# Two transformer-like layers in float32r on one core: first tile in two runs of chunks, the sum of phi(k) in float32r, accumulators added one by one

## Chip, cores and metric

The kernel runs on one core of a Trainium2 chip. The metric is the device time of one execution in microseconds (us). Three runs of the kernel before took 1350.85, 1351.03 and 1351.11 us; their median is 1351.03.

## What is computed

The input is one sequence of 2048 rows with 640 columns. Two kinds of block alternate, A, B, A, B, each on a layer-normalized copy and with a residual. A is linear attention with 32 heads of 20 columns; B is a feed-forward block of width 1728 with a squared ReLU.

```python
def _A_ref(x, wqkv, wo):
    q, k, v = split_heads(x @ wqkv)              # 32 heads of 20
    phi = lambda t: jnp.where(t > 0, t + 1, jnp.exp(t)) + 1e-6
    pq, pk = phi(q), phi(k)
    kv = jnp.einsum("bhsd,bhse->bhde", pk, v)
    z = jnp.einsum("bhsd->bhd", pk)              # the sum of phi(k)
    num = jnp.einsum("bhqd,bhde->bhqe", pq, kv)
    den = jnp.einsum("bhqd,bhd->bhq", pq, z)[..., None] + 1e-6
    return merge_heads(num / den) @ wo

def _B_ref(x, w1, b1, w2, b2):
    h = x @ w1 + b1
    r = jnp.where(h > 0, h, 0)
    return (r * r) @ w2 + b2

for _ in range(2):
    x = x + _A_ref(_layernorm(x), A_wqkv, A_wo)
    x = x + _B_ref(_layernorm(x), B_w1, B_b1, B_w2, B_b2)
```

## The kernel before

Rows are worked in 16 tiles of 128, columns in 5 chunks of 128. Most matmuls are in float32r. Every operand of these is split into a high part (float32r) and a low part (the rest), and a product is three matmuls, high with low, low with high, high with high (`mm3`, line 377). `split` (line 127) makes the high part on ScalarE (ACT) and the low part on VectorE (DVE).

**The order is written out by hand.** `tc.manual_schedule()` keeps each engine's instructions in the order in which the Python code issues them. All DMAs but one of the last tile stand in one queue, that of SyncE (SP). TensorE (PE) writes into the eight banks of PSUM, which the code hands out by number.

**Start of layer 0.** PE is kept busy with filler transposes (`warm`, line 521: 30, and 15 more behind the first tile's). Tile 0 is loaded, normalized (`a_stats`, `a_apply`; 1/sigma is made on GpSimd, POOL), transposed by PE (`a_trans`) and split (`xT_split`). Meanwhile `FirstLoads` (line 165) brings in the ten blocks of the k and q weights, five chunks of each, and splits each block as `step` asks for it. The first tile then has a loop of its own in stage A (line 681): for k and then for q, for each chunk, for each half of 320 columns, one `mm3`. Between, at q's chunk 2, PE transposes tile 1.

**Stage A.** For each tile the K and Q projections are made (`part`, line 460), phi is applied in `Phi` (line 471: `exp` on ACT, the rest on DVE in `rest`), phi(k) is split (`k_post`, line 645) and added up in `acc` on POOL, and PE multiplies it with the normalized input into G (`g_part`, five banks) and into GT (`gt_part`, in pairs of tiles, added up on DVE). For some tiles the q projection is put off (`LATE`, `late_q`). At the end of stage A the sum of phi(k) over the rows is a matmul of a 128x128 tile of ones with `acc`, in float32 (line 806); its result on all partitions, `zbc`, gives the denominators.

**Stage B and the feed-forward stage.** G is turned into one matrix per layer (`kv_make`, `m_make`), tiles 0 to 3 are finished, and then four groups of four tiles go through the feed-forward stage (line 1510). A step is one of 14 column blocks of a group: `fc1` (15 matmuls of 512 columns), `act` (ACT and DVE), and `fc2` of the step before (`fc2`, line 1114), which accumulates over the 14 steps in one bank for each tile (`a0` to `a3`) and one for the last 128 columns of all four (`as`, the strip). In the last step of a group the accumulators are added to the residual by DVE (`tile_add`, line 1106), and the next group's first matmul into such a bank waits for that. Work for the next groups' tiles hangs on places between these steps ("pre", 0 to 4, "pe", "post"); `single` (line 1379) lays it out for tiles 4 to 7, among it `f_bias` (line 631), which adds the second bias and stores the tile for the end of its group.

## Time and profile before

| | |
|---|---|
| runs | 1350.85, 1351.03, 1351.11 us |
| profiled execution | 1350.55 us |
| its span, from the first to the last instruction | 1348.6 us |
| DMA | 253.44 MB, mean 188 GB/s |

A row of the timeline has the start in us, the time from the first start to the last end in us, the engine, the line, the operation, what it writes and reads by the program's names, the shape and the count, and in brackets how long the engine was idle before and what ended that. PEld is the loading of weights into PE, SPq the issue of a DMA. In the view of waits a row has the waiting engine and line, what it waited for, the total in us, how often, and the longest. In a table by stretches of time each engine has its busy time and, with x, its number of instructions, and then the granted PE clock, the DMA share and GB/s. In the list of groups a row ends with the busy time in us and the mean of one instruction in ns, then the idle time before it.

### The profile page before, as it was taken

Reading aid. Unit: us, or ns where it says so; the run is one execution under the profiler, and the core shown is the slowest. Engines: PE = TensorE matmul, PEld = TensorE weight load, DVE = VectorE, ACT = ScalarE, POOL = GpSimd, SP = SyncE. Lnnn points to the kernel's source line nnn. Section 1 sums busy time; section 2 is a strip of 40 time slices with the busy share of each in tenths; the row PEclk is TensorE's granted clock in tenths of the full one; section 3 lists DMA queues with packets and bytes.
Section 4 is the critical chain, followed back from the end, with each engine's and each line's share of the span. In section 5 each row is a group of like instructions: output and inputs, shape, how many; then the busy total and the mean of one; then the engine's idle time right before and its main releaser. Section 6 shows DMA issues by size and latency. Waiting matters only on the chain.

```text
span 1348.6 us, 19071 instructions
## 1 busy us (share of the span) xinstructions
PE 1340.0 (99%) x6793; PEld 1157.7 (86%) x6793; DVE 914.9 (68%) x1631; ACT 796.9 (59%) x2021; POOL 122.6 (9%) x174
## 2 busy tenths in 40 slices
PE   9999999999999999999999999999999999999998
PEld 8888998988888888888888899988888888888887
DVE  7888757777776776643467676677778667766323
ACT  5888858566547447511647688485756466474120
POOL 2222210000000000000012232100000000000000
PEclk9999999999999999999999999999999999999999
DMA  6787824574654574487621114156546556545735
GB/s 205 254 295 270 287 91 167 191 287 136 216 205 161 200 263 166 154 298 291 224 98 49 50 40 150 47 206 247 175 164 228 179 176 224 208 163 181 252 128 194
DMA packets 85636, 253.44 MB, mean 188 GB/s; under 512 B 11030, under 2 KB 19606, under 8 KB 84902
## 3 DMA queue, kind: packets, MB, share of 16 engines
q1 hardware_dynamic: 85398, 252.04, 53.8%
q8 instruction: 54, 0.88, 0.3%
q14 instruction: 40, 0.33, 0.1%
q10 hardware_dynamic: 144, 0.20, 0.0%
HBM read 193.50 MB, written 56.03 MB: 185 GB/s over the span
## 4 chain that ended last, share of the span: by engine, by line
PE 89%; DVE 5%; ACT 3%; issue 1%; DMA 1%; POOL 0%; SPq 0%; DVEq 0%; ACTq 0%
PE PS L381 34%; PE PS L1057 27%; PE PS L1007 27%; ACT z L367 2%; PE PS L854 1%; PE PS L867 1%; DMA st<-in_A_wqkv_dram 0%; DVE bn L338 0%; DVE e L484 0%; DVE xr L623 0%; DVE r L485 0%; DVE xTb L130 0%; DMA Mr<-Mc 0%; POOL rs L343 0%; DVE y L358 0%
## 5 line engine op out<-in xcount | busy, mean ns | idle before, releaser
L367 ACT ACTIVATE z<-y 32x160 f32<-32x160 f32 x1424 | 475.8, 334 | 77.4 <-DVE y L358 61.2
L1007 PE MATMUL PS<-xTb,u 128*128 128x512 f32 x1400 | 333.1, 389 | 1.0 <-DVE xTb L130 1.0
L1007 PEld LDWEIGHTS PS<-xTb,u 128*128 128x128 f32 x1400 | 262.0, 188 | 55.3 <-DVE xTb L130 1.5
L381 PE MATMUL PS<-kq,xT 128*128 128x320 f32 (+2 forms) x1635 | 294.0, 334 | 1.4 <-DVE kq L130 0.9
L381 PEld LDWEIGHTS PS<-kq,xT 128*128 128x128 f32 x1635 | 259.0, 188 | 29.1 <-DVE kq L130 1.1
L1057 PE MATMUL PS<-u,h 128*128 128x512 f32 x1120 | 277.1, 390 | 0.3 <-DVE x L1108 0.3
L1057 PEld LDWEIGHTS PS<-u,h 128*128 128x128 f32 x1120 | 208.4, 188 | 41.9 <-DVE x L1108 1.2
L1019 ACT ACTIVATE hr<-PS,b1sb 128x512 f32<-128x512 f32 x104 | 71.4, 687 | 277.3 <-PE PS L1007 276.4
L1020 DVE TENSOR_TENSOR hr<-hr 128x512 f32<-128x512 f32 x104 | 71.8, 690 | 220.7 <-ACT hr L1019 220.3
L381 PE MATMUL PS<-kh,xh 128*128 128x512 f32 x480 | 124.3, 392 | 0.0
L477 ACT ACTIVATE e<-PS 128x320 f32<-128x320 f32 (+4 forms) x128 | 53.6, 435 | 102.6 <-PE PS L381 98.9
L342 POOL TENSOR_SCALAR rs<-mv 128x1 f32<-128x1 f32 x64 | 28.0, 438 | 869.8 <-DVE mv L340 869.8
L381 PE MATMUL PS<-uM,pT 128*128 128x320 f32 x648 | 102.6, 309 | 0.7 <-DVE uM L883 0.7
L381 PEld LDWEIGHTS PS<-uM,pT 128*128 128x128 f32 x648 | 97.7, 188 | 3.1 <-DVE uM L883 1.3
L381 PEld LDWEIGHTS PS<-kh,xh 128*128 128x128 f32 x480 | 87.3, 188 | 15.1
L484 DVE TENSOR_SCALAR e<-e 128x320 f32<-128x320 f32 (+4 forms) x128 | 41.2, 322 | 80.3 <-ACT e L477 80.0
L1057 PE MATMUL PS<-h,u 128*128 128x512 f32 x280 | 79.0, 390 | 0.0
L1022 DVE TENSOR_TENSOR h<-hr,h 128x512 fp32r<-128x512 f32 x104 | 72.0, 693 | 3.6
L652 POOL TENSOR_TENSOR acc<-acc,r 128x640 f32<-128x640 f32 x30 | 53.9, 1795 | 199.9 <-DVE r L485 199.9
L1057 PEld LDWEIGHTS PS<-h,u 128*128 128x128 f32 x280 | 52.1, 188 | 10.8 <-DVE h L1033 0.4
L1007 PE MATMUL PS<-xTb,uw 128*128 128x512 f32 x240 | 57.0, 389 | 0.0
L485 DVE SCALAR_TENSOR_TENSOR r<-PS,e 128x512 f32<-128x512 f32 (+2 forms) x104 | 51.1, 492 | 5.8 <-ACT e L477 2.4
(122 smaller groups left out, 1361.5 us busy)
## 6 DMA issues: line engine op xcount, KB each, us to landing
u<-kept_w SPq DMA_DIRECT2D x184, 640.0 KB, 4.5
x<-x SPq DMA_DIRECT2D x48, 320.0 KB, 4.8
kept_w<-uprep SPq DMA_DIRECT2D x23, 640.0 KB, 4.5
pqt<-pq SPq DMA_DIRECT2D x32, 320.0 KB, 4.6
x<-xr SPq DMA_DIRECT2D x32, 320.0 KB, 3.2
st<-in_B_w_dram SPq DMA_DIRECT2D x22, 320.0 KB, 5.9
pq<-r SPq DMA_DIRECT2D x20, 320.0 KB
kept_kq<-kq SPq DMA_DIRECT2D x10, 640.0 KB, 6.9
```

Source lines behind the costliest of these rows:

```text
L342: nc.gpsimd.tensor_scalar(rs, mv[:, 1:2], LN_EPS, None, op0=ALU.add)
L367: nc.scalar.activation(zv[j * B32 : (j + 1) * B32, :, i, :], yv[i * B32 : (i + 1) * B32, :, j, :], AF.Copy)
L381: nc.tensor.matmul(ps, a, b, start=first and i == 0, stop=last and i == 2)
L477: nc.scalar.activation(self.e[:, a:b], ps, AF.Exp)
L484: nc.vector.tensor_scalar(e, e, 1.0, PHI_EPS, op0=ALU.min, op1=ALU.add)
L485: nc.vector.scalar_tensor_tensor(out=self.r[:, a:b], in0=ps, scalar=0.0, in1=e, op0=ALU.max, op1=ALU.add)
L652: nc.gpsimd.tensor_tensor(out=acc, in0=acc, in1=r, op=ALU.add)
L1007: nc.tensor.matmul(ps, a[:, d, :], bb[:, d, :], start=d == 0 and i == 0, stop=d == DC - 1 and i == len(seq) - 1,)
L1019: nc.scalar.activation(r, ps, AF.Relu, bias=b1sb[:, c : c + 1])
L1020: nc.vector.tensor_tensor(out=r, in0=r, in1=r, op=ALU.mult)
L1022: nc.vector.tensor_tensor(out=h[:, 1], in0=r, in1=h[:, 0].bitcast(F32), op=ALU.subtract)
L1057: nc.tensor.matmul(ps, l, r, start=first and k == 0, stop=last and k == len(a) - 1)
```

## The change

Four edits are made together.

1. **The first tile in two runs of chunks.** Chunks 0 and 1, then 2 to 4, are normalized, transposed into two banks and split as separate instructions. There are 25 filler transposes instead of 30, and none behind the tile's transposes. The first tile's projections run chunk by chunk through k and q: the matmuls of both parts of the input with the weight's high part first, and those with the weight's low part two chunks later (`LAG`). Tile 1's transposes come at step 7 of this (`AT_T`), the first 512 columns of tile 1's projections at step 9 (`AT_P`), into bank 6. The statistics and normalizations of tiles 1 to 3, the last two q weights' splits and tile 2's transposes are moved accordingly.
2. **The sum of phi(k) in float32r.** `acc` is split like any operand, between the first two parts of the put-off q projections, and the sum is four float32r matmuls, the low part first, instead of two in float32. The tile of ones becomes float32r, written by DVE from a one-column constant, which shares a tile with the constant -0.5; POOL wrote it before.
3. **Accumulators added at once in a group's last step.** `tile_add` of a tile is issued right behind that tile's last `fc2` matmuls and not behind all four.
4. **The bias of tile 7** (`f_bias` for i = 3) comes one step later.

```diff
@@ -36,7 +36,10 @@
 LATE = ((9, 11, 12, 13, 14, 15), (8, 9, 11, 13, 14, 15))
 
 PREP = {t: 2 if t > 5 else 3 for t in range(2, 12)}
-N_WARM, N_WARM_2 = 30, 15
+N_WARM = 25
+
+
+LAG, AT_T, AT_P = 2, 7, 9
 AHEAD = 2
 F_BUFS = 12
 
@@ -107,7 +110,9 @@
 
     ident = cpool.tile([P, P], F32, name="ident")
     make_identity(nc, ident)
-    neghalf = cpool.tile([P, 1], F32, name="neghalf")
+    scalars = cpool.tile([P, 2], F32, name="scalars")
+    neghalf, one = scalars[:, 0:1], scalars[:, 1:2]
+    nc.vector.memset(one, 1.0)
     nc.vector.memset(neghalf, -0.5)
     b2bc = cpool.tile([P, D], F32, name="b2bc")
     b1sb = cpool.tile([P, NF], F32, name="b1sb")
@@ -169,16 +174,29 @@
             self.todo = [(nm, c) for nm in ("k", "q") for c in range(DC)]
             self.pending = []
 
+            self.halves = []
+
+        def high(self, n):
+            for _ in range(min(n, len(self.pending))):
+                (nm, c), raw = self.pending.pop(0)
+                if nm == "k":
+                    kq[c] = wtile("kq").rearrange("p (j n) -> p j n", j=2)
+                    keep(("kq", c), [P, 2, 2 * D])
+                s = slice(0, D) if nm == "k" else slice(D, 2 * D)
+                u = kq[c][:, :, s]
+                nc.scalar.activation(u[:, 0], raw, AF.Copy)
+                self.halves.append((u, raw))
+
+        def low(self, n):
+            for _ in range(min(n, len(self.halves))):
+                u, raw = self.halves.pop(0)
+                nc.vector.tensor_tensor(
+                    out=u[:, 1], in0=raw, in1=u[:, 0].bitcast(F32), op=ALU.subtract
+                )
+
         def finish(self):
-            if not self.pending:
-                return
-            (nm, c), raw = self.pending.pop(0)
-            if nm == "k":
-                kq[c] = wtile("kq").rearrange("p (j n) -> p j n", j=2)
-                keep(("kq", c), [P, 2, 2 * D])
-            s = slice(0, D) if nm == "k" else slice(D, 2 * D)
-            u = kq[c][:, :, s]
-            split(u[:, 0], u[:, 1], raw)
+            self.high(1)
+            self.low(1)
 
         def step(self, n=1, ahead=2):
             for i in range(n + 1):
@@ -527,18 +545,39 @@
             first_loads.step(0, 5)
             a_load(1, src)
             a_stats(0)
-            a_apply(0)
+            first_loads.high(2)
+
+            mv, rs = sts.pop(("a", 0))
+            T4[0] = tmp.tile([P, TG, 2, D], R32, tag="T", name="xT", bufs=2)
+            xT[0] = chunks(T4[0][:, 0])
+            runs = [(bank(4), 0, 2), (bank(5), 2, DC)]
+            for ps, a, b in runs:
+                v = xt[0][:, a * P : b * P]
+                nc.vector.tensor_scalar(v, v, mv[:, 0:1], rs, op0=ALU.subtract, op1=ALU.mult)
+            for ps, a, b in runs:
+                for c in range(a, b):
+                    nc.tensor.transpose(
+                        ps[:, (c - a) * P : (c - a + 1) * P], xt[0][:, c * P : (c + 1) * P], ident
+                    )
+                d = T4[0][:, 0, 0, a * P : b * P]
+                nc.scalar.activation(d, ps[:, : (b - a) * P], AF.Copy)
+            first_loads.low(1)
+            for ps, a, b in runs:
+                d = T4[0][:, 0, :, a * P : b * P]
+                nc.vector.tensor_tensor(
+                    out=d[:, 1], in0=ps[:, : (b - a) * P], in1=d[:, 0].bitcast(F32), op=ALU.subtract
+                )
+            first_loads.low(1)
             first_loads.step(2, 5)
-            a_trans(0, bank(4, 2))
-            warm(N_WARM_2)
-            first_loads.step(4, 5)
             a_stats(1)
+            first_loads.step(2, 5)
+            a_apply(1)
+            a_load(2, src)
             first_loads.step(1, 5)
-            a_apply(1)
-            first_loads.step(3, 5)
-            a_load(2, src)
-        ones = ap.tile([P, P], F32, name="ones", tag="ones", bufs=1)
-        nc.gpsimd.memset(ones, 1.0)
+            first_loads.high(1)
+            first_loads.low(1)
+        ones = ap.tile([P, P], R32, name="ones", tag="ones", bufs=1)
+        nc.vector.tensor_copy(ones, one.to_broadcast([P, P]))
         mask = ap.tile([HR, 6, DH], F32, name="mask", tag="mask", bufs=1)
         nc.gpsimd.memset(mask, 1.0)
 
@@ -680,26 +719,43 @@
                 load_vo(2 * t - 25)
             if first:
                 fk, fq = Phi(rtile()), Phi(rtile())
-                for nm, f, pss in (("k", fk, (bank(0), bank(1))), ("q", fq, (bank(2), bank(7)))):
-                    w = wk(nm)
-                    for c in range(DC):
+                pss = {"k": (bank(0), bank(1)), "q": (bank(2), bank(7))}
+
+                def first_part(nm, c, passes):
+
+                    x, w = xT[0][:, :, c, :], wk(nm)[c]
+                    for i in passes:
+                        k, l = ((0, 0), (1, 0), (0, 1))[i]
                         for j in range(2):
-                            s = slice(j * HD, (j + 1) * HD)
-                            mm3(
-                                pss[j][:, :HD], xT[t][:, 0, c, :], xT[t][:, 1, c, :],
-                                w[c][:, 0, s], w[c][:, 1, s], c == 0, c == DC - 1,
+                            nc.tensor.matmul(
+                                pss[nm][j][:, :HD], x[:, k], w[:, l, j * HD : (j + 1) * HD],
+                                start=c == 0 and i == 0, stop=c == DC - 1 and i == 2,
                             )
-                        if nm == "q" and c == 2:
-                            a_trans(1, bank(5, 2))
-                            a_stats(2)
-                            a_apply(2)
-                    for j in range(2):
-                        f.exp(j * HD, pss[j][:, :HD])
-                    if nm == "k":
-                        f.rest()
+
+
+                seq = [(nm, c) for nm in "kq" for c in range(DC)]
+                for n in range(len(seq) + LAG):
+                    if n < len(seq):
+                        first_part(*seq[n], (0, 1))
+                    if n >= LAG:
+                        first_part(*seq[n - LAG], (2,))
+                    if n == DC + LAG - 1:
+                        for j in range(2):
+                            fk.exp(j * HD, pss["k"][j][:, :HD])
+                    if n == AT_T:
+                        first_loads.high(2)
+                        a_trans(1, bank(4, 2))
+                        first_loads.low(2)
+                        a_stats(2)
+                        fk.rest()
+                    if n == AT_P:
+                        ps_first = part(1, 0, 512, bank(GB[3]))
+                for j in range(2):
+                    fq.exp(j * HD, pss["q"][j][:, :HD])
+                a_apply(2)
+                fq.rest()
                 xh[t] = split_new(xt[t], "xh")
                 k_post(t, fk.r)
-                fq.rest()
                 nc.sync.dma_start(pqd[0], fq.r)
                 continue
             g = list(range(DC)) if t > 0 else []
@@ -714,14 +770,15 @@
             is_late = t in late
             f, fq = Phi(rtile()), None if is_late else Phi(rtile())
             n0 = HD if is_late else 512
-            ps = part(t, 0, n0, bank(XB[0]))
+            ps = ps_first if layer == 0 and t == 1 else part(t, 0, n0, bank(XB[0]))
             gs(0 if is_late or t == 1 and layer == 0 else 2)
             move(t + 1)
             f.exp(0, ps)
-            if layer == 0 and t == 1:
+            second = layer == 0 and t == 1
+            if second:
+                f.rest()
                 a_stats(3)
-                a_trans(2, bank(5, 2))
-            if not early and t + 2 < NT:
+            elif not early and t + 2 < NT:
                 a_apply(t + 2)
                 yza[t + 2] = blocks_T(xt[t + 2])
             f.rest()
@@ -729,6 +786,10 @@
             ps = part(t, n0, D if is_late else 1024, bank(XB[1]))
             if t + 1 in yza:
                 xT_split(t + 1, yza.pop(t + 1)[1])
+            if second:
+                a_trans(2, bank(4, 2))
+                a_apply(3)
+                yza[3] = blocks_T(xt[3])
             if early:
                 xT_split(2, yz0[2][1])
             for _ in range(PREP.get(t, 0) if layer == 0 else 0):
@@ -799,11 +860,17 @@
                 if j == 1:
                     nc.sync.dma_start(pqd[t], late_phi.pop(t).r)
 
-        late_q(2)
+        late_q(1)
+        ah = xtile("ah")
+        split(ah[:, 0], ah[:, 1], acc)
+        late_q(1)
         zbc = tmp.tile([P, D], F32, tag="z", name="zbc", bufs=1)
         psz = [xbank()[:, :HD] for _ in range(2)]
         for j in range(2):
-            nc.tensor.matmul(psz[j], ones, acc[:, j * HD : (j + 1) * HD], start=True, stop=True)
+            for i in (1, 0):
+                nc.tensor.matmul(
+                    psz[j], ones, ah[:, i, j * HD : (j + 1) * HD], start=i == 1, stop=i == 0
+                )
         for j in range(2):
             nc.scalar.activation(zbc[:, j * HD : (j + 1) * HD], psz[j], AF.Copy)
         b_den(0)
@@ -1124,13 +1191,12 @@
                 after(0)
                 for i in range(TG):
                     fc2_tile(g, c, h, i)
+                    tile_add(g, i)
                     if i < TG - 1:
                         after(i + 1)
                 if not beside:
                     strip_turn(g)
                 after(TG)
-                for i in range(TG):
-                    tile_add(g, i)
                 if beside:
                     strip_blocks(g)
                 else:
@@ -1410,7 +1476,7 @@
             at(b, "pe", out)
             at(b + 1, "pre", add)
             at(b + 1, "post", lambda: blocks_move(yzx[t], (0, 1)))
-            at(b + 1 + 2 * (i == 3), "post", lambda: f_bias(t))
+            at(b + 1 + 3 * (i == 3), "post", lambda: f_bias(t))
             at(b + 2, "pre", lambda: blocks_move(yzx[t], (2, 3)))
             steps(at, lambda: x_split(t), (b + 2, "post"), (b + 2, "post"))
```

## The prediction

> **What bounds the kernel now.** I read the page first (busy time, then the chain that ended last), then what TensorE (PE) waited for, then the timeline at the three places that the change touches.
>
> ```profile
> span 1348.6 us, 19071 instructions
> PE 1340.0 (99%) x6793; PEld 1157.7 (86%) x6793; DVE 914.9 (68%) x1631; ACT 796.9 (59%) x2021; POOL 122.6 (9%) x174
> PE 89%; DVE 5%; ACT 3%; issue 1%; DMA 1%; POOL 0%; SPq 0%; DVEq 0%; ACTq 0%
> ```
>
> PE is busy for 1340.0 of 1348.6 us and carries 89% of the chain. So an edit pays in three ways only: it lets PE start its real matmuls sooner, it takes away one of the few stalls, or it takes work off PE. The view of PE's waits has one near a microsecond:
>
> ```profile
> PE PS L381 <- DVE kq L130: 0.9, 1, 0.9
> ```
>
> It is in the first tile. The start, from the timeline:
>
> ```profile
> 5.86 0.61 DVE L348 TENSOR_SCALAR xt<-xt,mv,rs 128x640 f32<-128x640 f32 x1 [1.00 <-POOL rs L343]
> 6.53 0.77 PE L352 MATMUL PS<-ident,xt 128*128 128x128 f32 x5
> 7.13 1.80 PE L523 MATMUL PS<-ident 128*128 128x128 f32 x15
> 7.33 0.71 ACT L129 ACTIVATE xT<-PS 128x640 fp32r<-128x640 f32 x1 [1.25 <-PE PS L352]
> 8.69 6.54 PE L381 MATMUL PS<-kq,xT 128*128 128x320 f32 x42
> 10.48 4.07 ACT L129 ACTIVATE kq<-st 128x640 fp32r<-128x640 f32 x5 [0.57 <-DMA st<-in_A_wqkv_dram]
> 14.46 0.75 ACT L477 ACTIVATE e<-PS 128x320 f32<-128x320 f32 x2
> 14.59 0.61 DVE L348 TENSOR_SCALAR xt<-xt,mv,rs 128x640 f32<-128x640 f32 x1 [0.77 <-POOL rs L343]
> 15.12 2.48 DVE L130 TENSOR_TENSOR kq<-st,kq 128x640 fp32r<-128x640 f32 x3
> 16.09 1.15 PE L381 MATMUL PS<-kq,xT 128*128 128x320 f32 x6 [0.86 <-DVE kq L130]
> 21.87 0.98 DVE L348 TENSOR_SCALAR xt<-xt,mv,rs 128x640 f32<-128x640 f32 x1 [0.99 <-POOL rs L343]
> 23.22 0.71 PE L352 MATMUL PS<-ident,xt 128*128 128x128 f32 x5
> ```
>
> The first real matmul is at 8.69, behind 15 filler transposes, though its left operand is ready at 8.04. After 42 matmuls PE waits for the low part of the third q weight, since VectorE (DVE) does the splits late: it waited 0.77 us for the second tile's 1/sigma.
>
> **Start of the first tile.** The whole-tile normalization (0.61) becomes two pieces, 256 and 384 columns. Bounds for these: a 256-wide ScalarE (ACT) read of PSUM and DVE pieces of 256 and 384 in
>
> ```profile
> 34.43 0.38 ACT L477 ACTIVATE e<-PS 128x256 f32<-128x256 f32 x1
> 34.99 0.29 DVE L484 TENSOR_SCALAR e<-e 128x256 f32<-128x256 f32 x1
> 31.27 0.56 DVE L485 SCALAR_TENSOR_TENSOR r<-PS,e 128x384 f32<-128x384 f32 x1
> 188.74 4.56 PE L381 MATMUL PS<-kq,xT 128*128 128x320 f32 x30
> ```
>
> The normalization row has two operands per partition and is slower than L484's, so I take 0.38 and, begun 0.07 before that ends, 0.45: ends at 6.24 and 6.62. A signal to PE takes 0.06 (6.47 to 6.53): two transposes from 6.30. Five of them bring ACT on 0.80 after their start (6.53 to 7.33); three fewer at 0.11 save 0.3, so ACT's high part of that run goes from 6.79 to 7.18 (0.38) and the first matmul starts at 7.24: 1.45 earlier, as no filler stands ahead of it. Its low part (DVE, 0.42, behind the first k weight's) is there at 7.71. A 320-wide matmul takes 0.147 (the last row: 30 in 4.40, up to the next instruction at 193.14, quoted below). The new order issues 38 of them for k with the first two q weights: 5.6 us, plus 0.15 waiting at 7.71 for the first low part and about 0.25 for slow restarts (the six behind the wait at 16.09 take 1.15 where 0.88 and the last one's drain are due), ends near 13.0. Loads don't move: SyncE's (SP's) order is unchanged there, and the q weights' high parts run as they land (10.48, 4.07 for five). Two of these now stand behind the two exponentials of k (0.75 for both): 13.25 to 13.9, then 13.9 to 15.28, and the second tile's high part to 15.89. PE meets them almost as it comes: it is through the first tile and the first 512 columns of the second at 20.84, where it was at 23.22 before. **PE alone would be 2.4 us ahead.**
>
> That lead can't be kept, because DVE is full here. In both orders DVE reaches the last two q weights' splits or, after, the second tile's low part at about the same time: before at 15.12 + 0.84 = 15.96 (a third of the x3 row), after at 15.93 (it waits for ACT's 15.89). From there to the first phi of tile 1 it does the same list. Before:
>
> ```profile
> 30.68 0.29 DVE L485 SCALAR_TENSOR_TENSOR r<-PS,e 128x128 f32<-128x128 f32 x1
> 34.30 0.77 DVE L655 TENSOR_TENSOR kh<-r,kh 128x640 fp32r<-128x640 f32 x1
> 35.82 1.52 PE L381 MATMUL PS<-kh,xh 128*128 128x512 f32 x6
> 45.20 0.48 DVE L513 COPY GT<-PS 128x320 f32<-128x320 f32 x1
> 46.21 3.57 PE L381 MATMUL PS<-kq,xT 128*128 128x512 f32 x15
> ```
>
> 15.96 to 30.68 is 14.72, with 0.99 idle for POOL's 1/sigma (row at 21.87). After, the statistics of tile 2 stand ahead of k's phi, whose four instructions cover that wait. So DVE is done 1.0 to 1.2 us earlier, not 2.4; ACT's next work hangs on that phi and gains the same. PE meets DVE at two places: tile 1's low K (before 35.07, used 35.82, slack 0.7 with a signal's 0.06) and the copy of GT (45.68, used 46.21, slack 0.47). The lead that is left is DVE's plus the smaller slack: 1.17 + 0.47 = 1.64. **I take 1.6.** Bounds: 0.8 (DVE gains 0.8, which is the 0.99 less the new constant copy and one more piece, and no slack helps) and 2.3 (DVE keeps up). From tile 3 on DVE has idle time again, so the lead stays to the end.
>
> The moved transposes (0.46 for tile 2) are only paid later. The new 128x128 constant on DVE (about 0.2, between 0.06 of a one-column memset and 0.77 of a 640-wide pass) falls into its wait for ACT before 15.93; it leaves POOL's queue, where nobody waited. Where that cover is missing it costs its 0.2.
>
> **Sum of phi(k).**
>
> ```profile
> 185.31 3.59 PE L381 MATMUL PS<-kh,xh 128*128 128x512 f32 x15
> 186.98 2.01 POOL L652 TENSOR_TENSOR acc<-acc,r 128x640 f32<-128x640 f32 x1 [5.67 <-DVE r L485]
> 191.13 0.44 ACT L477 ACTIVATE e<-PS 128x320 f32<-128x320 f32 x1 [3.53 <-PE PS L381]
> 191.97 0.49 DVE L485 SCALAR_TENSOR_TENSOR rl<-PS,e 128x320 f32<-128x320 f32 x1
> 193.14 1.24 PE L806 MATMUL PS<-acc,ones 128*128 128x320 f32 x4
> 193.97 3.85 PE L381 MATMUL PS<-kh,xh 128*128 128x512 f32 x15
> ```
>
> Two float32 matmuls show as four entries: 0.83 to the next start, and the 15 behind them take 3.85 against 3.59: together 1.09. Four float32r matmuls at 0.147 make 0.59: 0.50 less per layer. Against it stands a new wait: the sum is split on ACT (from 191.47, 0.74) and DVE (from 192.4, behind L485, 0.82), and the first new matmul takes the low part, ready at 193.26 where PE comes at 193.14. That is 0.12 and about 0.1 of restart: net 0.27 per layer, **0.55 for both** (bounds 0 and 1.0). POOL's last addition is done at 188.99, so the split doesn't wait for it. Behind DVE's new instruction the next one waits for ACT until 193.8; nobody is delayed. The tile takes one slot of a ring of eight; what comes to lie in its slot is written some 20 us later.
>
> **Accumulators, and the bias of tile 7.**
>
> ```profile
> 369.69 0.78 DVE L634 TENSOR_TENSOR xr<-xr,b2bc 128x640 f32<-128x640 f32 x1
> 369.94 3.56 PE L1007 MATMUL PS<-xTb,u 128*128 128x512 f32 x15
> 372.18 0.82 DVE L1259 TENSOR_TENSOR pT<-z,pT 128x640 fp32r<-128x640 f32 x1
> 372.92 2.48 DVE L1108 TENSOR_TENSOR x<-PS,x 128x512 f32<-128x512 f32 x4
> 373.65 3.05 PE L1057 MATMUL PS<-u,h 128*128 128x512 f32 x12 [0.15 <-DVE x L1108]
> 1039.85 3.05 PE L1057 MATMUL PS<-u,h 128*128 128x512 f32 x12 [0.15 <-DVE x L1108]
> ```
>
> 15 matmuls take 3.43 undisturbed (185.31 to 188.74), here 3.71 up to the next start, and the 12 behind 2.90 to the start of the next three where 2.75 is due: the stall costs 0.28 + 0.15 = 0.43. The bias addition (0.78) goes behind the step and two additions ahead of pT's split (0.82): the first addition ends 1.5 us sooner, at 372.1, and PE comes at 373.37. The rest follow at 0.6 each, PE at 0.69. So **0.86 for both layers** (bounds 0 and 0.9). In groups 1 and 2 the order on DVE doesn't change, as nothing stood between. On SP the store of tile 7 now comes behind two weight loads; it holds the third until about 376.3, three microseconds later than now, for weights used three steps ahead.
>
> **Sum.** 1.6 + 0.55 + 0.86 = 3.0. The profiled execution took 1350.55 (span 1348.6 and 1.95 around it): 1347.5. The median of the runs, 1351.03, is 0.48 above it: **1348.0 us.**
>
> **Rivals.** *The lead is kept whole* (DVE isn't the bound in tiles 1 and 2): 2.3 + 0.55 + 0.86, at 1347.3. For it: two slacks in which the early work may hide; against it the unbroken DVE list.
>
> *The start gains least:* 0.8, and the phi split costs what it saves: 1.66 in all, 1349.4. For it: each hand-over in the first 8 us is a wait for another engine, and POOL's 1/sigma for tile 1 now runs beside DVE's splits, which no row shows.
>
> *The clock falls back.* The filler is 25 transposes, ends near 5.9 and leaves PE idle in pieces up to 7.24.
>
> ```profile
> 1.40:5.00 3.60, 3.58 (x17) 3.59 (x18) 1.10 (x3) 1.14 (x2) 0.05 (x1) 1.00 0.89 284
> 5.00:8.60 3.60, 3.60 (x34) 3.47 (x33) 2.61 (x4) 2.27 (x5) 0.74 (x2) 1.00 0.94 339
> ```
>
> PE did 17 in the first 3.6 us and 34 in the next, so a second slow spell would cost half of 3.6, 1.8; the lead of PE would be 0.6 instead of the 1.6 that DVE allows: 1349.0. Against it: about 0.6 us idle in all is little of 3.6. The Trainium skill (TensorE: Matmul & The Clock Gate, Part 4: PE-mode transpose) says that transposes don't count as PE activity for the clock; by that rule the filler would be worthless in both kernels and this rival likely. The trace disagrees: nothing but transposes ran up to 5.0, and the pace doubled there.
>
> *PE's pace changes:* slower. The tiles behind the sum of phi sit one slot further in their ring; if another placement made PE's reads slower, then 0.9 ns on each of 6793 matmuls (6.1 us) outweighs the gain and 2.7 more, giving 1354; from 0.45 ns on there is no gain. Against it: the two layers have other buffers and keep one pace (the stall rows at 373.65 and 1039.85 lie 666.20 apart, the phi rows of the two layers 666.18).
>
> *It doesn't do what it says:* the additions still wait (an operand load) and the stall stays: 2.15, at 1348.9.
>
> **How the numbers follow.** Forecast 0.55 (own range 1347.2 to 1348.8), lead kept 0.16, least gain 0.14, clock 0.05, pace 0.05, stall stays 0.05. Range: from 1346.8 (every upper bound, 4.2) less the 0.26 between the three runs, so 1346.5, to 1349.9 (the start at 0.8, the sum of phi at 0 and a third of the last term: 1.1). 0.2% is 2.7 us, about what a measurement here can tell from none: that is 1348.33, inside the forecast's range. I count 0.40 of its 0.55 as faster and the 0.16 of the kept lead, some 0.02 of the rest: 0.58; slower is the pace rival, 0.05; no change 0.37.
>
> **What would show it.** Right: the first 320-wide matmul near 7.2; no PE wait for kq as long as 0.9; small waits for DVE at the low K of tile 1 or at GT; four float32r matmuls in about 0.6 behind a wait near 0.1; no wait for x in the group's last step. Wrong: 17 slow entries again behind 6 us; DVE idle between 16 and 30; a mean per matmul in the feed-forward rows other than 389 ns, as in
>
> ```profile
> L1007 PE MATMUL PS<-xTb,u 128*128 128x512 f32 x1400 | 333.1, 389 | 1.0 <-DVE xTb L130 1.0
> ```

## The result, and the profile after

The changed kernel takes **1348.61 us** (median of 22 runs, 1348.16 to 1349.34); the kernel before takes 1350.91 beside it (22 runs, 1350.49 to 1351.40). The ratio is 0.9984, with a 95% interval of 0.9977 to 0.9990. So 2.3 us went, where 3.0 were forecast. The profiled execution took 1348.58 us.

From the page of the changed kernel: span, busy time, the chain that ended last, and one row of the groups (busy us, mean ns).

```profile
span 1346.6 us, 19032 instructions
PE 1338.8 (99%) x6773; PEld 1155.9 (86%) x6773; DVE 916.6 (68%) x1638; ACT 797.7 (59%) x2024; POOL 123.3 (9%) x172
PE 92%; ACT 3%; DVE 3%; DMA 1%; issue 1%; POOL 0%; SPq 0%; DVEq 0%; ACTq 0%
L1074 PE MATMUL PS<-xTb,u 128*128 128x512 f32 x1400 | 333.3, 390 | 1.0 <-DVE xTb L135 1.0
```

The span is 2.0 shorter, and PE's share of the chain went from 89 to 92%. The pace of PE is the same (390 ns for 389), so the gain was made in single places. To find them I take the same matmul in both traces: the start before less the start after is PE's **lead**. It stays level over long stretches and steps at few places:

| PE's lead over the kernel before, us | at 62 | 190 | 200 | 372.5 | 374.5 | 380 | 850 | 863 | 1038.5 | 1041 | end |
|---|---|---|---|---|---|---|---|---|---|---|---|
| changed kernel | 0.96 | 0.96 | 1.26 | 1.27 | 1.71 | 1.47 | 1.46 | 1.78 | 1.81 | 2.26 | 2.01 |

(The first row has the time in the kernel before.) The three terms can be read off. The start gave 0.96, forecast 1.6. The sum of phi gave 0.30 + 0.32 = 0.62, forecast 0.55. The group ends gave 0.44 and 0.45, as forecast, and lost 0.24 and 0.25 of it at once: 0.40 net, forecast 0.86.

The timeline of the changed kernel at the start:

```profile
5.95 0.80 DVE L556 TENSOR_SCALAR xt<-xt,mv,rs 128x256 f32<-128x256 f32 x2 [1.00 <-POOL rs L361]
6.78 0.74 ACT L187 ACTIVATE kq<-st 128x640 fp32r<-128x640 f32 x1 [1.42 <-DMA st<-in_A_wqkv_dram]
7.42 0.75 ACT L563 ACTIVATE xT<-PS 128x256 fp32r<-128x256 f32 x2
7.84 6.89 PE L730 MATMUL PS<-kq,xT 128*128 128x320 f32 x44 [0.46 <-ACT xT L563]
10.92 2.40 ACT L187 ACTIVATE kq<-st 128x640 fp32r<-128x640 f32 x3 [0.87 <-DMA st<-in_A_wqkv_dram]
...
11.92 1.52 DVE L193 TENSOR_TENSOR kq<-st,kq 128x640 fp32r<-128x640 f32 x2
...
12.86 1.00 POOL L361 TENSOR_TENSOR rs<-rs,scalars 128x1 f32<-128x1 f32 x1
13.74 0.77 ACT L495 ACTIVATE e<-PS 128x320 f32<-128x320 f32 x2 [0.42 <-PE PS L730]
13.90 0.61 DVE L366 TENSOR_SCALAR xt<-xt,mv,rs 128x640 f32<-128x640 f32 x1 [0.47 <-POOL rs L361]
...
16.39 0.82 DVE L135 TENSOR_TENSOR xT<-PS,xT 128x640 fp32r<-128x640 f32 x1
...
21.11 0.60 DVE L366 TENSOR_SCALAR xt<-xt,mv,rs 128x640 f32<-128x640 f32 x1
```

The two normalization pieces are done by 6.75, near the 6.62 worked out. But the first 320-wide matmul comes at 7.84, not 7.24: ACT's next work is the second k weight, whose load landed only at 6.78, and the tile's high part stands behind that, at 7.42. (The filler was late too: the tile's first transpose stood behind it until 6.67. In t1_behind, a run below, ACT follows the first transpose by 0.42, which here would be 7.09, so the weight was the later of the two.) In the profile of before this weight was on ACT at 5.34, the second of the pair in

```profile
4.53 1.55 ACT L129 ACTIVATE kq<-st 128x640 fp32r<-128x640 f32 x2 [2.46 <-DMA st<-in_A_wqkv_dram]
```

The first q weight is on ACT at 10.92, where it was at 10.48.

The timeline of the changed kernel at the sum of phi, and at the end of a group:

```profile
191.41 0.82 DVE L135 TENSOR_TENSOR ah<-acc,ah 128x640 fp32r<-128x640 f32 x1
192.28 0.59 PEld L871 LDWEIGHTS PS<-ah,ones 128*128 128x128 f32 x4 [0.21 <-DVE ah L135]
192.28 0.85 PE L871 MATMUL PS<-ah,ones 128*128 128x320 f32 x4
```

```profile
367.64 0.84 DVE L376 STREAM_TRANSPOSE y<-pqt 128x640 f32<-128x640 f32 x1
370.17 1.28 DVE L1175 TENSOR_TENSOR x<-PS,x 128x512 f32<-128x512 f32 x2
370.69 4.14 ACT L385 ACTIVATE z<-y 32x160 f32<-32x160 f32 x12
372.07 2.88 PE L1124 MATMUL PS<-u,h 128*128 128x512 f32 x12
374.86 0.69 ACT L1086 ACTIVATE hr<-PS,b1sb 128x512 f32<-128x512 f32 x1
375.60 2.38 PEld L1074 LDWEIGHTS PS<-xTb,u 128*128 128x128 f32 x11 [0.39 <-ACT hr L1086]
```

Two additions now run from 370.17, well ahead of the matmuls at 372.07, which have no wait. (These are the first `fc2` of the next group, into the same banks. The prediction and some expectations call them the group's last step; the matmul that waited is the same.) But behind the fifteen matmuls of that step PE waits again, in front of the weights at 375.60. The bank that it wants to write is still being read by ACT's activation (374.86 to 375.55), and that comes only behind twelve block copies.

### The profile page after: what moved, and what is told of

Same layout as the page of the kernel before. It is cut to its first block, busy times and chain, and to the rows that moved or that the text cites. A ratio compares the mean times of both kernels' runs of the same rounds, so it can differ in the third digit from the quotient of the medians.

```text
span 1346.6 us, 19032 instructions
## 1 busy us (share of the span) xinstructions
PE 1338.8 (99%) x6773; PEld 1155.9 (86%) x6773; DVE 916.6 (68%) x1638; ACT 797.7 (59%) x2024; POOL 123.3 (9%) x172
## 4 chain that ended last, share of the span: by engine, by line
PE 92%; ACT 3%; DVE 3%; DMA 1%; issue 1%; POOL 0%; SPq 0%; DVEq 0%; ACTq 0%
PE PS L399 34%; PE PS L1074 28%; PE PS L1124 28%; ACT z L385 2%; PE PS L921 1%; PE PS L934 1%; PE PS L730 1%; DVE bn L356 0%; DMA st<-in_A_wqkv_dram 0%; DVE xr L662 0%; DVE e L502 0%; DVE xTb L135 0%; DMA Mr<-Mc 0%; DVE r L503 0%; POOL rs L361 0%
## 5 line engine op out<-in xcount | busy, mean ns | idle before, releaser
L399 PE MATMUL PS<-kq,xT 128*128 128x320 f32 (+2 forms) x1575 | 284.4, 334 | 0.4 <-DVE GT L533 0.4
L399 PEld LDWEIGHTS PS<-kq,xT 128*128 128x128 f32 x1575 | 250.1, 188 | 28.1 <-DVE rl L503 1.0
L1124 PEld LDWEIGHTS PS<-h,u 128*128 128x128 f32 x280 | 52.2, 188 | 10.8 <-DVE h L1100 0.4
```

Source lines behind the costliest of these rows:

```text
L399: nc.tensor.matmul(ps, a, b, start=first and i == 0, stop=last and i == 2)
L1124: nc.tensor.matmul(ps, l, r, start=first and k == 0, stop=last and k == len(a) - 1)
```

## The experiments

Theory A: the start is held by the landing of the weights and then by DVE, and at the group's end a part of the gain is lost again to ACT's queue. All were timed against the kernel before on the same chip:

| kernel | median, us | before, us | less by | ratio, 95% interval |
|---|---|---|---|---|
| start_alone | 1349.69 | 1350.99 | 1.30 | 0.9982 to 1.0 |
| phi_alone | 1350.55 | 1350.99 | 0.44 | 0.9988 to 1.0006 |
| adds_alone | 1350.73 | 1350.99 | 0.26 | 0.9989 to 1.0006 |
| moves_behind | 1349.85 | 1350.99 | 1.14 | 0.9983 to 1.0001 |
| t1_behind | 1347.96 | 1350.97 | 3.01 | 0.9969 to 0.9987 |
| lag_one | 1349.70 | 1350.97 | 1.27 | 0.9982 to 0.9999 |
| constant_seven | 1349.99 | 1350.97 | 0.98 | 0.9983 to 1.0001 |
| no_filler | 1350.12 | 1350.97 | 0.85 | 0.9982 to 1.0 |
| k_first | 1348.46 | 1350.99 | 2.53 | 0.9975 to 0.9992 |
| stats_early | 1348.71 | 1350.99 | 2.28 | 0.9975 to 0.9993 |
| both_ahead | 1348.28 | 1350.99 | 2.71 | 0.9972 to 0.9990 |
| all_four | 1347.53 | 1350.99 | 3.46 | 0.9967 to 0.9985 |

An interval is some 2.4 us wide, so a few tenths between two variants aren't told by it. Where the text names tenths, it rests on the lead of PE in the traces, with the medians beside it.

### Each part alone

start_alone has the first tile's parts of the diff and leaves the constant on POOL:

```diff
+            first_loads.high(2)
...
+            runs = [(bank(4), 0, 2), (bank(5), 2, DC)]
...
+                    if n == AT_P:
+                        ps_first = part(1, 0, 512, bank(GB[3]))
```

phi_alone has

```diff
+        ah = xtile("ah")
+        split(ah[:, 0], ah[:, 1], acc)
...
+            for i in (1, 0):
+                nc.tensor.matmul(
+                    psz[j], ones, ah[:, i, j * HD : (j + 1) * HD], start=i == 1, stop=i == 0
+                )
```

with the constant in float32r. adds_alone has

```diff
                     fc2_tile(g, c, h, i)
+                    tile_add(g, i)
...
-                for i in range(TG):
-                    tile_add(g, i)
...
-            at(b + 1 + 2 * (i == 3), "post", lambda: f_bias(t))
+            at(b + 1 + 3 * (i == 3), "post", lambda: f_bias(t))
```

> The kernel before with the first-tile edit alone (the pieces, the order of the matmuls and of VectorE's work; the sum of phi, the additions and the bias as before). Theory A, read from the changed kernel's trace: the edit is worth 1.0 in the span, and no more, since the first real matmul can't begin before ScalarE has copied the second k weight, which it takes ahead of the tile and whose load lands late; 1.0 less than before at the end, the lead of TensorE about 2.0 at 21 us and 1.0 behind 45 us. Rival B, the prediction's ledger: 1.6, the rest of the shortfall lying in the edits' meeting with each other; the lead behind 45 us is then near 1.6 here. If the pace of the first transposes doubles near 5.0 us as before, and not near 6.4 as in the changed kernel, the late rise belongs to one execution and not to the edit.

> The kernel before with the sum of phi(k) in float32r alone, its constant made on VectorE. Both the prediction and the changed kernel's trace say 0.55 to 0.6 for both layers, so 0.5 to 0.6 less time. Rival: what the changed kernel gained between 180 and 208 us came with its earlier VectorE, and alone the edit gives 0.2 or nothing.

> The kernel before with the additions moved and tile 7's bias shifted, nothing else. Theory A: the stall of 0.45 in front of the group's last step goes in both layers, but TensorE then reaches the next group's bank while ScalarE still reads it (it comes to that read only after twelve block copies), a new wait of 0.26 each: 0.4 less in all, and the new wait shows in front of the matmuls at about 376.9 and 1043.1. Rival B, the prediction's 0.86: the new wait in the changed kernel came from elsewhere (its early VectorE or the start's lead) and isn't seen here.

The medians give 1.30, 0.44 and 0.26, together 2.0 against 2.30 for all; the intervals can't tell these apart. The lead of each over the profile of before shows that each edit's steps are the same alone as together, so the edits hardly act on each other:

| PE's lead, us | at 62 | 190 | 200 | 372.5 | 374.5 | 380 | 850 | 863 | 1038.5 | 1041 | end |
|---|---|---|---|---|---|---|---|---|---|---|---|
| start_alone | 1.11 | 1.11 | 1.11 | 1.12 | 1.13 | 1.17 | 1.17 | 1.17 | 1.19 | 1.20 | 1.23 |
| phi_alone | -0.83 | -0.83 | -0.54 | -0.51 | -0.50 | -0.47 | -0.47 | -0.15 | -0.13 | -0.13 | -0.11 |
| adds_alone | -0.82 | -0.80 | -0.80 | -0.80 | -0.36 | -0.62 | -0.62 | -0.62 | -0.60 | -0.15 | -0.42 |

phi_alone steps by 0.29 and 0.32: the term is right. adds_alone gains 0.44 and gives back 0.26 within six microseconds, in both layers, with nothing else changed. Its timeline, at the place where theory A saw the new wait (here 0.8 later, as the start was):

```profile
372.76 4.15 ACT L367 ACTIVATE z<-y 32x160 f32<-32x160 f32 x12
376.94 0.69 ACT L1019 ACTIVATE hr<-PS,b1sb 128x512 f32<-128x512 f32 x1
377.68 1.01 PEld L1007 LDWEIGHTS PS<-xTb,u 128*128 128x128 f32 x5 [0.39 <-ACT hr L1019]
```

So the new wait belongs to the edit, and the ledger's 0.86 (rival B) is out. start_alone keeps a lead of 1.11, near theory A's 1.0 and not the ledger's 1.6 (the landing, below, has its part in that).

The left column is the surprise. phi_alone and adds_alone have the start of the kernel before, yet are 0.82 behind its profile at 62. Their first q weight reached ACT at 11.07 and 11.28, and it did at 10.48 in that profile; their second k weight came at 6.84 and 6.87, for 5.34. **The profile of before caught an early landing of the weights.** This is taken up below.

### The new wait at the group's end

```diff
-                    at(s + (pl + k) // 5, (pl + k) % 5, lambda t=t, k=k: blocks_move(yzp[t], (k,)))
+                    n = 5 if (p, k, t) == (0, 3, t0) else pl + k
+                    at(s + n // 5, n % 5, lambda t=t, k=k: blocks_move(yzp[t], (k,)))
```

> The changed kernel with the last four of those twelve block copies of ScalarE placed behind the activation that frees the next group's bank, in each place where a group of four tiles hands over to the next in this way. Theory A: the activation starts 1.4 earlier, at about 373.5, the new wait of 0.26 is gone in both layers, and the time is 0.4 to 0.5 below the changed kernel's, the span near 1346.1. Rival: the next wait stands just behind (the copies are late for the split that follows, or TensorE waits for the low part that VectorE makes), and the gain is below 0.2.

It was slower than the changed kernel by 1.2. The four copies that it moves are those of the pair's first tile, from a step earlier: they came into the crowded step instead of out of it. In a table by stretches, ACT (the fourth pair) is busy for 9.14 of these 10 us, where it is for 7.93 in the changed kernel:

```profile
366.00:376.00 10.00, 9.83 (x44) 7.85 (x43) 8.76 (x16) 9.14 (x24) 0.00 (x0) 1.00 0.69 275
```

PE lost another 0.17 there and 0.46 at the next hand-over between groups, in both layers. As a test it shows the sign: more copies ahead of the activation, more wait. t1_behind moves the right ones, with `t1` for `t0` in the diff above.

> The changed kernel with ScalarE's last four block copies of the second tile of the pair (the ones that really stand ahead of the activation at 374.86) placed behind that activation; moves_behind had moved four others, from an earlier step into this one, and so lengthened the queue. Theory A: the activation starts 1.4 earlier, the wait of 0.26 in front of the matmuls at 375.60 and 1041.26 is gone, the time 0.4 to 0.5 below the changed kernel's, so near 2.8 below the kernel before. Rival: the pair's split is late in its place, or VectorE's low part, and the gain is below 0.2.

Measured: 3.01 below the kernel before. The changed kernel was 2.30 below, so 0.7 more. Its timeline:

```profile
372.97 0.69 ACT L1086 ACTIVATE hr<-PS,b1sb 128x512 f32<-128x512 f32 x1
373.68 1.37 ACT L385 ACTIVATE z<-y 32x160 f32<-32x160 f32 x4
374.95 1.30 PE L1074 MATMUL PS<-xTb,u 128*128 128x512 f32 x5
375.08 0.53 ACT L1323 ACTIVATE pT<-z 128x384 fp32r<-128x384 f32 x1
```

The activation is done 1.3 us before PE comes to its bank, and the wait is gone. Against the kernel before the lead now steps from 1.79 to 2.27 and from 2.62 to 3.11, so 0.48 and 0.49, with nothing given back. Theory A holds here; the rival (the pair's split is late) doesn't show.

### What holds the start

```diff
-        nc.vector.tensor_copy(ones, one.to_broadcast([P, P]))
+        for _ in range(7):
+            nc.vector.tensor_copy(ones, one.to_broadcast([P, P]))
```

> The changed kernel with VectorE's copy that makes the 128x128 constant done seven times instead of once, 0.8 to 1.3 more work on VectorE at 16.1, just ahead of tile 1's low part. Theory A: VectorE's unbroken list from there to 31 us sets the lead, so the time rises by 0.7 to 1.3, less what waits for POOL at 28.0 take up (0.31). Rival: TensorE's own late start sets the lead, VectorE has slack, and the time rises by less than 0.3.

The median is 1.4 above the changed kernel's, and in the trace PE's lead is 1.2 smaller from 18 us to the end. The timeline shows the place:

```profile
15.44 0.71 ACT L134 ACTIVATE xT<-PS 128x640 fp32r<-128x640 f32 x1
15.89 1.79 DVE L581 CAST ones<-scalars 128x128 fp32r<-128x128 f32 x7
17.59 0.82 DVE L135 TENSOR_TENSOR xT<-PS,xT 128x640 fp32r<-128x640 f32 x1
18.47 0.73 PE L399 MATMUL PS<-kq,xT 128*128 128x512 f32 x2 [1.23 <-DVE xT L135]
```

One copy fits in the wait for ACT, six more don't: tile 1's low part begins 1.20 later than in the changed kernel, and 1.20 is missing at the end. (The first q weight came 0.21 earlier here, at 10.71; with that taken off, the copies cost the 1.4 of the medians.) DVE has no slack from this place on, and the rival, in which PE's late start sets the lead, is out.

The next question is what sets when DVE begins this list. lag_one brings the low passes closer behind the high ones, so that k doesn't wait for the second q weight:

```diff
-LAG, AT_T, AT_P = 2, 7, 9
+LAG, AT_T, AT_P = 1, 7, 9
```

> The changed kernel with the first tile's low passes one unit behind the high ones instead of two, so that the last k weight's pass needs the first q weight's high part (ScalarE done at 11.66), not the second's (12.49). Theory A: the first tile is held by the landing of the weights, so k is complete near 13.0 instead of 13.69, its exponentials begin when ScalarE is through with the third q weight (13.31, not 13.74), and tile 1's transposed copy, VectorE behind it and the end come 0.3 to 0.4 earlier. Rival: VectorE's low parts are then late for TensorE (a PE wait for kq) or VectorE's own list sets the lead; no gain, or up to 0.2 lost.

It was 1.1 slower than the changed kernel, by the rival's mechanism but far more of it. PE's rows:

```profile
14.96 0.57 PE L730 MATMUL PS<-kq,xT 128*128 128x320 f32 x2 [0.63 <-DVE kq L193]
18.46 0.56 PE L730 MATMUL PS<-kq,xT 128*128 128x320 f32 x2 [0.92 <-DVE kq L193]
```

The lag of two keeps PE from q's low parts until DVE has them; with one, the kind of wait that the change had removed (0.9 for kq) is back, as 0.63 and 0.92. The next three shorten the chains into tile 1's low part without that. k_first has the lag of one for k alone:

```diff
-                    if n >= LAG:
-                        first_part(*seq[n - LAG], (2,))
-                    if n == DC + LAG - 1:
+                    for m, (nm, c) in enumerate(seq):
+                        if m + (1 if nm == "k" else LAG) == n:
+                            first_part(nm, c, (2,))
+                    if n == DC:
```

> The changed kernel with the low passes of k one unit behind the high ones and those of q two behind as they were (lag_one, mended: there the low passes of q came to TensorE before VectorE had them). Theory A': two chains of equal length meet at tile 1's low part (16.39): ScalarE's, held to 13.74 by the exponentials of k and done at 16.35, and VectorE's, held to 13.90 by POOL's power and done at 16.30. This edit shortens ScalarE's alone by 0.43, so the time stays within 0.15 of the changed kernel's. Rival: ScalarE's chain alone sets it; 0.4 less.

stats_early moves the statistics of tile 1:

```diff
-            first_loads.step(2, 5)
+            first_loads.step(1, 5)
             a_stats(1)
-            first_loads.step(2, 5)
+            first_loads.step(3, 5)
```

> The changed kernel with tile 1's statistics one weight split earlier on VectorE, so that POOL's addition and power (1.69 for both beside VectorE's splits) are done before the normalization is due. It takes away VectorE's wait of 0.47 in front of 13.90 and nothing else. Theory A': alone within 0.15 of the changed kernel's time, as ScalarE's chain is still there at 16.35. Rival: VectorE's list alone sets the lead; 0.4 less.

both_ahead has both edits.

> k_first and stats_early together. Theory A': both chains are 0.4 shorter, so tile 1's low part begins near 15.95 and the end comes 0.3 to 0.45 earlier than in the changed kernel, more than the two alone add up to. Rival: something else holds the start (the landing of the weights at TensorE, say), and the three runs lie within 0.15 of the changed kernel's.

Alone each stays within 0.25 of the changed kernel's gain (2.53 and 2.28 for 2.30), where A' had 0.15; together 2.71. The medians can't settle it, and the landing moves too, so the traces are compared with that taken off, one for one (t1_behind, with a landing 0.55 earlier, had this low part 0.55 earlier, at 15.84). Tile 1's low part began 0.23, 0.19 and 0.45 earlier than at 16.39, in executions whose first q weight came 0.13, 0.07 and 0.26 earlier: 0.10, 0.12 and 0.19 are left for the edits. That is a sum and not more, and half of the 0.4. (In all_four below, which has both edits too, 0.14 is left, so even these figures carry some hundredths of scatter.) The timeline of both_ahead shows why:

```profile
11.71 2.64 PEld L730 LDWEIGHTS PS<-kq,xT 128*128 128x128 f32 x18 [0.34 <-DVE kq L193]
13.05 0.68 DVE L366 TENSOR_SCALAR xt<-xt,mv,rs 128x640 f32<-128x640 f32 x1
14.46 0.71 PE L370 MATMUL PS<-ident,xt 128*128 128x128 f32 x5
15.20 0.71 ACT L134 ACTIVATE xT<-PS 128x640 fp32r<-128x640 f32 x1
15.94 0.82 DVE L135 TENSOR_TENSOR xT<-PS,xT 128x640 fp32r<-128x640 f32 x1 [0.53 <-ACT xT L134]
```

The tile is normalized by 13.73, 0.8 earlier, and PE turns it only at 14.46, when it comes to that place in its order: a third chain of nearly the same length. A part of it the edits made themselves: PE waits at 11.71 for the low part of a k weight, which with both edits comes to be needed while DVE still has the statistics ahead of it; the changed kernel has no such wait there. This is an inconclusive test of A' and a fair account of why the start resists: three engines meet at one tile.

### The filler

```diff
-N_WARM = 25
+N_WARM = 0
```

> The changed kernel without its 25 filler transposes. In the profiles so far the pace of the transposes doubled after 3.6 to 5.1 us of nothing but transposes. Theory A: they count, so without them the first real work, from 6.4, runs at half pace up to 10 to 11.5; 320-wide matmuls at 0.267 instead of 0.147 put TensorE 1.4 to 2.5 behind, and since the lead is 1 behind 45 us the time rises by 1.0 to 2.0. Rival: transposes don't count (the rule that the prediction named); the clock rises in any case with the first real matmuls or by itself, and the time is the changed kernel's within 0.3.

The median is 1.5 above the changed kernel's; in the trace PE's lead is 1.0 smaller, with the first q weight 0.29 earlier (10.63). A table by stretches of PE's busy time and count, in the changed kernel and then without the filler:

```profile
7.40:11.00 3.60, 3.16 (x20) 3.00 (x21) 3.27 (x7) 2.73 (x7) 0.00 (x0) 1.00 1.04 400
11.00:14.60 3.60, 3.60 (x27) 3.50 (x25) 3.10 (x7) 3.00 (x6) 2.35 (x4) 1.00 1.04 400
```

```profile
7.40:11.00 3.60, 3.60 (x15) 3.55 (x14) 3.25 (x6) 2.73 (x5) 0.00 (x0) 1.00 1.02 383
11.00:14.60 3.60, 3.60 (x27) 3.60 (x26) 3.10 (x7) 1.85 (x3) 2.37 (x4) 1.00 1.04 402
```

Without filler PE's first work is at 6.29, and it runs at half pace up to 10.8: 0.267 from one 320-wide matmul to the next, 0.147 afterwards. Fifteen matmuls are done in the first stretch though PE never idles. With the filler all real matmuls run at full pace. The granted clock (the third figure from the end) reads 1.00 in all rows; the pace has to be read from the counts. So work of transposes alone does raise PE's pace here. The Trainium skill (TensorE: Matmul & The Clock Gate, Part 4: PE-mode transpose) says that they don't count as PE activity for the clock. By that this run should have lost nothing; it lost 1.5, and the measurement decides. (The page speaks of a transpose mode; the rows here say MATMUL and don't show the mode.)

### All together

all_four is both_ahead with t1_behind, and in the sum of phi the high part first:

```diff
-            for i in (1, 0):
+            for i in (0, 1):
                 nc.tensor.matmul(
-                    psz[j], ones, ah[:, i, j * HD : (j + 1) * HD], start=i == 1, stop=i == 0
+                    psz[j], ones, ah[:, i, j * HD : (j + 1) * HD], start=i == 0, stop=i == 1
```

> both_ahead, t1_behind and the high part before the low one in the sum of phi(k) (the low part is then ready when TensorE comes to it; 0.1 to 0.2 per layer less). If the terms add: 0.4, 0.65 and 0.3 below the changed kernel, near 1347.3; if the gain of the start is eaten by VectorE's next waits, near 1347.7.

It has the lowest median of all, 1347.53: 3.46 below the kernel before, and 1.1 below the changed kernel's median. Against the changed kernel's trace the lead steps by 0.14 and 0.12 at the two sums of phi, by 0.28 and 0.28 at the two group ends, and the start has 0.29, of which 0.22 is an earlier landing. Whether it beats t1_behind (1347.96) can't be told from the intervals.

## Why the prediction was right, and where it was off

**The start, 1.6 forecast, 0.96 in the profile.** Its working was sound but for one input: it let the weights land when they had in the profile of before ("the q weights' high parts run as they land (10.48, 4.07 for five)"). In the trace of the changed kernel the second k weight was on ACT 1.44 later and the first q weight 0.44 later, and k, which was to be complete near 13.0, let its exponentials begin only at 13.74, not at 13.25. (The 13.0 is a slip in the sum: 7.24, 5.6, 0.15 and 0.25 make 13.2, which is what the 13.25 behind it needs.) From several executions (starts of rows; the lead is over the profile of before; "phi of tile 1" is the 128-wide piece that completes its phi(k), which the prediction calls the first phi):

| kernel | first q weight on ACT | exponentials of k | phi of tile 1 on DVE | lead at 62 |
|---|---|---|---|---|
| before | 10.48 | 14.46 | 30.68 | 0 |
| phi_alone | 11.07 | 15.03 | 31.81 | -0.83 |
| adds_alone | 11.28 | 15.25 | 31.48 | -0.82 |
| changed kernel | 10.92 | 13.74 | 30.02 | 0.96 |
| t1_behind | 10.37 | 13.19 | 29.49 | 1.49 |

t1_behind has the changed kernel's start and an early landing, near that of before. Its timeline:

```profile
6.00 0.74 ACT L187 ACTIVATE kq<-st 128x640 fp32r<-128x640 f32 x1 [0.77 <-DMA st<-in_A_wqkv_dram]
7.29 6.89 PE L730 MATMUL PS<-kq,xT 128*128 128x320 f32 x44
10.37 2.38 ACT L187 ACTIVATE kq<-st 128x640 fp32r<-128x640 f32 x3 [0.72 <-DMA st<-in_A_wqkv_dram]
```

There the steps come out as worked out: the first matmul at 7.29 (7.24), the phi at 29.49 (30.68 less 1.17 is 29.51), the lead 1.49 (1.64). DVE gains what was forecast: its wait of 0.99 for tile 2's 1/sigma (21.87 before) is gone, as the row at 21.11 above shows. (The 1.17 itself isn't worked out there: 0.99 and the 0.03 from 15.96 to 15.93 make 1.02. The 1.19 here is 1.07 less time from tile 1's low part at 15.84 to this phi, and 0.12 of earlier begin.) The slack on top is 0.30 (1.49 less 1.19) where 0.47 was counted; in the changed kernel it is 0.30 as well (0.96 less 0.66). The landing differs between executions of one order of loads, by up to 0.55 for the new start (10.37 to 10.92) and 0.8 for the old. Comparing two single profiles therefore mixes the edit with the landing. With the medians, which take many landings, the start alone was worth 1.30. The rest of the missing 0.3 is within the interval.

**POOL's 1/sigma beside DVE's splits**, which by the prediction "no row shows", took 1.00 for the power where the other rows have 0.57 to 0.59 (a row of before did show the other half of 1/sigma so: the addition at 13.21 took 0.69 beside a weight's split, 0.23 at 4.95), and cost DVE a wait of 0.47 at 13.90. stats_early takes that wait away and gains about 0.1, so it isn't the step that failed.

**The sum of phi, 0.55 forecast.** The mechanism and the size were right: 0.62 in the profile, 0.61 in phi_alone. The wait for the low part is there and as small as worked out; all_four shows that it is worth another 0.13 per layer, for the order of the parts alone.

**The group ends, 0.86 forecast, 0.40 measured. This is the step that failed.** The stall of 0.43 was sized right (0.44 and 0.45) and went. The prediction then asked only what DVE and SP do behind the moved bias. It didn't follow PE to its next hand-over: behind the fifteen matmuls of the step PE needs the bank that ACT frees, and ACT's queue, twelve copies of 0.34, hadn't moved. With four copies out of the way (t1_behind) the term measures 0.97, and the three terms in that execution, 1.49, 0.61 and 0.97, make the 3.1 by which its span is shorter. So the whole of the term can be had, but not by the edit as it was made.

**The rivals.** *The lead is kept whole*: out, since constant_seven shows DVE as the bound. *The start gains least*: out as a whole; the start's 0.96 is near its bound of 0.8 for another reason (the landing), and phi didn't cost what it saved. *The clock falls back*: the slow pace lasted longer, through 24 of the 25 filler transposes up to 6.5 instead of 17 up to 5.0, but no real matmul was slow. *PE's pace changes*: out, the lead is level between the steps. *It doesn't do what it says*: out for the stall. The stall's place was taken by another wait, which was on no list. By the number alone this rival (1348.9) lies nearer to the 1348.61 than the forecast (1348.0) does, so the total doesn't tell them apart; the traces do. The result lies in the forecast's own range (1347.2 to 1348.8) with 0.2 to spare, although the group ends came out at half.

Of the signs named beforehand: no PE wait for kq as long as 0.9, right; small waits of PE at tile 1's low K (0.43 in front of the weights at 34.48, for DVE) and at GT (0.40 at 45.14, for which the profile names no engine), right; the four matmuls of phi behind a short wait, right; no wait for x in the step behind the additions, right; the first 320-wide matmul near 7.2, wrong in this execution (7.84) and right in t1_behind. Of the signs against: DVE is idle between 16 and 30 for 0.31 (at 28.32) and nothing longer, where it was for 0.99 and 0.31 before; of the slow transposes two begin behind 6 us, not 17; the mean per matmul is 390 for 389.

## What to carry to other kernels

When a stall is taken away, walk the engine on to its next two or three hand-overs and ask of each whether that engine's queue has moved too; here more than half of the gain was lost again fifteen matmuls further on, to copies that could be put elsewhere. Times read from one profile of a start that hangs on DMA carry that execution's landing: before they are used as absolute times, look at a second execution, or compare only what follows the landing. Where several engines meet at one tile, shortening one chain shows the next one, so measure the chains before choosing.

## What the runs showed of the hardware

- **The pace of PE doubles at a time that differs from execution to execution.** In thirteen executions that begin with the filler at 1.41, transposes follow each other by 0.213 at first and by 0.109 later; the first at full pace came between 4.6 and 7.0 us, after 15 to 26 slow ones. It made little difference to the end: start_alone (4.6) and the changed kernel (6.56) differ by 0.15 at 62, 0.06 of it landing. The filler takes up this spread. What sets the time, no run here shows.
- **A power of 128 numbers on POOL took 1.00 beside DVE's split of a weight and 0.57 to 0.59 otherwise**, in every trace with the new order. The Trainium skill (SBUF — State Buffer, Who interferes with whom) says that a DVE instruction with two SBUF inputs contends with a GpSimd instruction that reads SBUF, and that the lock on the ports they share is exclusive. The trace agrees in kind: the power (12.86 to 13.86) meets a DVE split with both inputs in SBUF that ends at 13.44, and ends 0.42 behind it, 0.15 less than its own 0.57; beside the split of tile 2, which reads PSUM (27.23 to 28.00), it took 0.57. In the kernel before DVE was idle beside it.
- **The same loads, issued in the same order, landed up to 0.8 us apart** between executions (first q weight on ACT between 10.48 and 11.28 with the old order). What makes them land early or late wasn't settled.
